# A batch's ranks follow its logits by four steps in place of ten, and its sends stand five steps apart

## The chip, the core and the metric

The kernel runs on one core of a Trainium2 chip. The core has five engines that each work through a queue of their own in order: TensorE (PE, with its weight loads as PEld), VectorE (DVE), ScalarE (ACT), GpSimd (POOL) and SyncE (SP). They wait for each other by semaphores. An instruction that waits holds everything behind it in its queue. Sixteen DMA engines move data for all of them. The metric is the device time of one execution, in microseconds; the times of a kernel are given as the median of several runs, with the lowest and the highest.

## The reference

Attention over 8 batches, 8 heads, 576 tokens and a head width of 64, in which scores more than tau below a row's maximum are dropped, and behind it a layer of 8 experts, of which each token goes to the one with the largest logit.

```python
scores = scale * np.matmul(q, k.transpose(0, 1, 3, 2))
thresh = np.max(scores, axis=-1, keepdims=True) - tau
scores = np.where(scores >= thresh, scores, -1000000000.0)
...
x = np.ascontiguousarray(attn_out.transpose(0, 2, 1, 3)).reshape(B * S, H * D)
logits = x @ w_gate
expert_idx = np.argmax(logits, axis=1)
...
for e in range(E):
    mask = expert_idx == e
    xe = x[mask]
    h = np.maximum(xe @ w1[e], 0.0)
    out[mask] = gate_w[mask, None] * (h @ w2[e])
```

## The kernel before

**Stages.** Attention runs over 32 pairs of heads (four pairs are a batch), ten steps to a pair; the loop `one_step` writes out, step after step, what each engine is to do, and the order of each engine's queue is this order. In step t of pair n, TensorE makes one tile of transposed scores (`st_unit`, L444), a piece of the product with v for the pair before (`av_rest`, `av_wide`), and one tile of plain scores for the pair after the next (`s_unit`, L388). VectorE reduces each plain tile to its row maxima (L411, L404) and masks each transposed tile (L481, L463); ScalarE takes exponentials (L478, L462) and rounds (L488); GpSimd makes the low halves (`pl`, L489). When the maxima of a pair are complete, VectorE takes their minimum (`r`, L418), TensorE transposes it (`pst`, L423, at the front of step 2) and ScalarE and VectorE split it into rows that go into CQ by DMA.

**What sets the order.** `after(k, f, where)` (L251) puts a piece of work k steps later, into one of four places of that step: FRONT, BET (after the transposed scores), MID (after the plain scores), END. `chain` (L258) spreads a list two to a step, `dense` (L263) three to a step. `phase(p, least)` (L254) gives the first distance of at least `least` steps that ends at step p of a pair.

**Logits, ranks and sends.** About 25 steps after a batch's last evacuation, at step 6 of a pair, `logits` (L670) makes the batch's logits on TensorE (32 matmuls for four tiles of tokens, 40 where a fifth tile holds the last 64 tokens of two batches), into `lg`. One step later `route` (L688) starts: eight VectorE pieces (L704 to L712) find each token's expert as a one-hot tile `oh` and add to the running counts `run`. `ranks` (L732) stands nine steps after `route`, at step 6 of the next pair: five or six matmuls turn `oh`, and the counts before this batch, into each token's place among its expert's tokens (`rk`), and seven VectorE pieces (L744 to L753) make of it the row number `posi` and the gate's denominator `sm`; `gate` (L728) writes the gate into the rows. Six steps after the ranks the first of the batch's sends follows (L760): an indirect DMA of GpSimd that writes 128 rows of `R` (or `Rh`, the fifth tile) to `xs` in DRAM at the rows of `posi`. The sends of batches 0 to 4 stand four steps apart, those of batch 5 two.

**Buffers around it.** `ps_m` (tag `m`) is one bank of PSUM: `pst` of every pair, `lg` and `rk` of every batch use it in turn, each after all readers of the one before. `R` has two buffers, so a batch writes its rows (L613, L610) into the one that the sends of two batches ago read. After each odd batch a lone tile (`lone`, L636) is divided and rounded on GpSimd (xnh L572, Rh L647) and transposed on SyncE's queue (L663).

**Behind attention** come the experts: rows are fetched from `xs` by tables made of the counts, and TensorE works through two matrix products per group of rows. The first tables (`tables0`) and fetches follow batch 5.

Of the kernel before, what the change touches and what calls it, by code (L numbers as in the profile page):

```python
# [15 lines left out]
ALU = mybir.AluOpType  # L16
# [4 lines left out]
B, H, S, D = 8, 8, 576, 64  # L21
# [26 lines left out]
TUNE = dict(  # L48
    lgp=6, rkp=6, hi=4, lo=5, rd=5, lead=10, r0=2, rs=1, r2=1, pl=0, pa=3, q0=1, qd=1, lgs=2, rks=2, c1=2, c3=1, c5=1, sl=10, ll=13, sp0=8, sps=0, lv=-9, sv=5, t0=16, av=2, tr=4, d=4, lg=5, d5=2, d6=2, d7=1, lg7=22, km=16, rate=15, dh=1, do=3, w1d=5, xv=3, so=0, sto=0, ord=0, sc=5, fa=3, fd=4, wa1=-70, w2=38, wa2=-86, wl1=-28, wl2=-6, avb=2, route=1, ranks=7, pp=8, ew=4, maskat=0, w1a=-35, w0=14, w1b=3,
)  # L50
# [3 lines left out]
def kernel(  # L54
# [196 lines left out]
    def after(k, f, where=END):  # L251
        plan(now[0] + k, f, where)

    def phase(p, least):  # L254

        return least + (p - now[0] - least) % NSTEP if now[0] + least < KM else least
# [431 lines left out]
    def route(b, n, dist, Lj, w, got):  # L688
# [6 lines left out]
        def t2(nm, dt=F32):  # L695
# [6 lines left out]
        nc.scalar.copy(was, run)  # L702
        (dense if b == B - 1 else chain)(0, [
            lambda: nc.vector.tensor_reduce(mx, Lj, axis=AX.X, op=ALU.max),  # L704
# [27 lines left out]
        def ranks():  # L732
# [4 lines left out]
            for i in range(n - 1):  # L737
# [5 lines left out]
            pos, total = (rk[:, z:z + n].unsqueeze(2) for z in (128, 136))  # L743
            after(0, lambda: tt(ps, rkv, base_e.unsqueeze(1).to_broadcast(bc), ALU.add), END)  # L744
            fs = [
                lambda: nc.vector.tensor_reduce(total, ex, axis=AX.X, op=ALU.add),
# [8 lines left out]
                lambda: gate(b, n),  # L755
            ]
            (dense if b == B - 1 else chain)(1, fs)

            def send(j):
                dma = nc.gpsimd.indirect_dma_start(  # L760
                    xs[:, :], bass.IndirectOffsetOnAxis(ap=posi[:, j:j + 1].bitcast(U32), axis=0), row(b, j), None
                )
                tc.declare_no_dep(dma.ins, group="xs", reason="each row of xs is written once, and read later")
                tc.add_to_no_dep_group("xs", dma.ins)
                sends.append(dma.ins)
                sent.add((b, j))
# [3 lines left out]
            for j in range(n):  # L770
                after(6 + dist * j, lambda j=j: send(j))

        after(phase(TUNE["rkp"], TUNE["ranks"]), ranks, TUNE["rks"])


# [511 lines left out]
    at = []  # L1287
# [200 lines left out]
```

## Time and profile before

| | |
|---|---|
| median of 3 runs | 914.24 us (906.66 to 915.16) |
| profiled execution | 911.92 us, of it 910.2 us span |
| TensorE clock granted over the span | 0.997 |
| TensorE busy | 872.8 us (96%) |
| VectorE, ScalarE, GpSimd busy | 638.2, 614.6, 547.1 us |
| HBM read and written | 90.56 and 19.17 MB |

Attention takes the first 500 us or so, the experts the rest. In the views below, times are microseconds from the start of the span; a row of the timeline gives an instruction's start, its length, its engine and line, what it writes and reads, and in square brackets how long the engine stood idle ahead of it and what ended that. The matmuls' ends are modelled, so their starts say more than their lengths.

### The profile page before, as it was taken

To read this page: it belongs to the slowest core of one execution; us is meant where nothing else is said; L and a number is where in the kernel's file an instruction comes from. 1 tells how busy PE (TensorE), PEld (TensorE's weight loads), DVE (VectorE), ACT (ScalarE), POOL (GpSimd) and SP (SyncE) were. 2 spreads that over 40 slices of the span, in tenths; PEclk is the share of its full clock that TensorE was granted. 3 is DMA by queue.
4 is the path that set the end of the run, shared out by engine and by line. 5 is a ranking of instruction groups with operands and counts; after the bars stand their busy time and mean duration, and the time that the engine had idled before them with its cause. 6 is when DMAs were issued, how large, how long until landed. Compare 5 with 4: busy or idle time off the path is not lost.

```text
span 910.2 us, 25378 instructions
## 1 busy us (share of the span) xinstructions
PE 872.8 (96%) x10047; PEld 626.9 (69%) x10047; DVE 638.2 (70%) x1322; ACT 614.6 (68%) x1074; POOL 547.1 (60%) x471
## 2 busy tenths in 40 slices
PE   4899999999999999999999999999999999999996
PEld 1377777777777677777777867676666666667773
DVE  7999999989899899898988746745334251524551
ACT  4799999989999899999889624453334252433561
POOL 7578888998989889989889634323222122221132
PEclk9999999999999999999999999999999999999999
DMA  8555666666866767867457785999755664646540
GB/s 198 142 126 124 152 145 150 163 160 144 202 149 166 161 149 167 170 149 187 110 146 191 190 193 181 314 302 339 189 174 160 185 190 144 192 146 218 188 168 27
DMA packets 176981, 158.16 MB, mean 174 GB/s; under 512 B 133273, under 2 KB 149147, under 8 KB 176860
## 3 DMA queue, kind: packets, MB, share of 16 engines
q1 hardware_dynamic: 156028, 105.39, 45.8%
q0 software_dynamic: 8992, 29.18, 10.2%
q10 hardware_dynamic: 11840, 21.94, 9.0%
q8 instruction: 80, 1.31, 0.6%
q14 instruction: 41, 0.34, 0.1%
HBM read 90.56 MB, written 19.17 MB: 121 GB/s over the span
## 4 chain that ended last, share of the span: by engine, by line
PE 36%; issue 5%; DMA 5%; POOL 4%; DVE 2%; ACT 2%; SPq 1%; ACTq 0%; POOLq 0%; DVEq 0%
PE h L380 16%; PE y L380 15%; DMA out_dram<-o,gt 2%; DMA xs<-R,posi 1%; POOL out_dram L1122 1%; DMA vf<-in_v_dram 1%; SPq L663 1%; DMA wf<-in_w_dram 1%; POOL xs L760 1%; POOL pl L493 1%; PE st L450 1%; PE s L395 1%; PE s L399 1%; PE st L380 1%; POOL xn L572 0%
## 5 line engine op out<-in xcount | busy, mean ns | idle before, releaser
L489 POOL TENSOR_TENSOR pl<-e,ph 128x1024 f16<-128x1024 f32 x93 | 198.6, 2136 | 51.3 <-ACT ph L488 45.4
L411 DVE TENSOR_REDUCE nm<-s 128x1 f32<-128x512 f32 (+1 forms) x320 | 199.9, 634 | 9.5 <-PE s L399 7.9
L380 PE MATMUL y<-wb,hl 128*128 128x512 f16 (+2 forms) x1104 | 196.3, 347 | 0.9 <-DVE hl L1071 0.8
L380 PEld LDWEIGHTS <-wb 128*128 128x128 f16 x2304 | 182.9, 98 | 19.7 <-issue 1.5
L975 DVE SCALAR_TENSOR_TENSOR wb<-wf,wb 128x1024 f16<-128x1024 f32 x96 | 119.4, 1276 | 73.5 <-ACT wb L972 70.7
L380 PE MATMUL h<-xT,wb 128*128 128x256 f16 (+3 forms) x1632 | 160.8, 260 | 0.3 <-issue 0.3
L380 PEld LDWEIGHTS <-hl 128*128 128x128 f16 (+2 forms) x1104 | 89.0, 98 | 98.9 <-DVE hl L1071 1.4
L481 DVE SCALAR_TENSOR_TENSOR e<-st,e 128x512 f32<-128x512 f32 x192 | 129.8, 676 | 23.4 <-ACT e L478 23.1
L395 PE MATMUL s<-QK 128*128 128x512 f16 (+3 forms) x640 | 133.1, 291 | 12.5 <-POOL QK L137 8.0
L450 PE MATMUL st<-QK 128*128 128x512 f16 (+3 forms) x640 | 136.0, 288 | 4.2 <-DVE e L481 2.0
L972 ACT ACTIVATE wb<-wf 128x1024 f16<-128x1024 f32 x96 | 98.3, 1053 | 60.0 <-DMA wf<-in_w_dram 46.7
L399 PE MATMUL s<-ck,CQ 128*128 128x512 f16 (+3 forms) x640 | 137.4, 290 | 0.0
L478 ACT ACTIVATE e<-st,ntau 128x512 f32<-128x512 f32 x192 | 132.3, 692 | 7.3 <-PE st L380 3.9
L1122 POOL DMA_INDIRECT out_dram<-o,gt x39 | 44.6, 1143 | 147.3 <-ACT o L1119 138.5
L380 PE MATMUL st<-CQ,ck 128*128 128x512 f16 (+3 forms) x640 | 131.1, 286 | 1.1 <-DMA CQ<-ptT 1.0
L541 PEld LDWEIGHTS av<-vf,e 128*128 128x128 f32 x512 | 91.8, 190 | 19.6
L462 ACT ACTIVATE e<-st,ntau_f 128x512 f32<-128x512 f32 (+1 forms) x160 | 92.3, 608 | 13.8 <-PE st L380 9.5
L488 ACT CAST ph<-e 128x1024 f16<-128x1024 f32 x93 | 96.6, 1038 | 5.9 <-issue 3.2
L1070 ACT ACTIVATE hl<-h 128x512 f16<-128x512 f32 (+2 forms) x78 | 43.6, 573 | 80.6 <-PE h L380 78.5
L561 PE MATMUL av<-vop,pl 128*128 128x65 f16 x768 | 97.2, 194 | 0.5 <-issue 0.5
L560 PE MATMUL av<-vop,ph 128*128 128x64 f16 x768 | 97.0, 193 | 0.3 <-issue 0.3
L562 PE MATMUL av<-vop,ph 128*128 128x65 f16 x768 | 96.0, 193 | 0.7 <-issue 0.7
(234 smaller groups left out, 1538.0 us busy)
## 6 DMA issues: line engine op xcount, KB each, us to landing
wf<-in_w_dram SPq DMA_DIRECT2D x96, 512.0 KB
QK<-z SPq DMA_DIRECT2D x124, 144.0 KB
qkf<-in_qk_dram ACTq DMA_DIRECT2D x29, 576.0 KB
vf<-in_v_dram SPq DMA_DIRECT2D x31, 320.0 KB
ck<-z SPq DMA_DIRECT2D x62, 72.0 KB
CQ<-z ACTq DMA_DIRECT2D x58, 72.0 KB
xT<-R SPq DMA_TRANSPOSE x153
x<-in_qk_dram SPq DMA_DIRECT2D x6, 288.0 KB
```

Source lines behind the costliest of these rows:

```text
L380: x = nc.tensor.matmul(*a, **kw).ins
L395: nc.tensor.matmul(sc[rows, oc], d["QA"][a][:, cols], d["KB"][a][:, CH[c]], start=True, stop=False)
L399: nc.tensor.matmul(sc[rows, oc], d["CQ"][:, at:at + cols.stop - cols.start], d["CK"][a][:, CH[c]], start=False, stop=True,)
L411: nc.vector.tensor_reduce(o, sc[:, 0:width(t)], axis=AX.X, op=ALU.max, negate=True)
L450: nc.tensor.matmul(sc[rows, oc], d["KB"][a][:, cols], d["QA"][a][:, CH[c]], start=True, stop=False)
L478: nc.scalar.activation(pf, sc, AF.Exp, bias=ntau, scale=0.125 / SS)
L481: masks.append(nc.vector.scalar_tensor_tensor(pf, sc, 0.0, pf, ALU.is_ge, ALU.mult).ins)
L489: nc.gpsimd.tensor_tensor(l, pd, h, ALU.subtract)
L560: nc.tensor.matmul(av[:, a, 0:D], h, vop[:, tv, W:W + D], start=False, stop=False)
L561: nc.tensor.matmul(av[:, a], l, vop[:, tv, 0:W], start=False, stop=False)
L972: high = nc.scalar.activation(o[:, :, 0], x, AF.Copy, scale=SW)
L975: low = nc.vector.scalar_tensor_tensor(o[:, :, 1], x, SW, o[:, :, 0], ALU.mult, ALU.subtract)
```

## The change

Four things move, for batches 0 to 5 (`soon`); nothing is computed otherwise.

- `route` writes its eight pieces three to a step in place of two, in every batch.
- The ranks stand three steps after `route` (`phase(0, 3)`), at step 0 of the next pair, behind its first transposed scores: four steps after the logits in place of ten.
- Their eight VectorE and ScalarE pieces stand in the order 0, 1, 2, 4, 6, 3, 5, 7 within this step and the next, instead of over four steps.
- The first send stands four steps after the ranks in place of six, and the others five steps apart (batch 5: four) in place of four (two).

```diff
-    ... tr=4, d=4, lg=5, d5=2, d6=2, ...
+    ... tr=4, d=5, lg=5, d5=4, d6=2, ...
...
-        (dense if b == B - 1 else chain)(0, [
+        dense(0, [
...
-            after(0, lambda: tt(ps, rkv, base_e.unsqueeze(1).to_broadcast(bc), ALU.add), END)
-            fs = [
+            fs = (
+                lambda: tt(ps, rkv, base_e.unsqueeze(1).to_broadcast(bc), ALU.add),
                 lambda: nc.vector.tensor_reduce(total, ex, axis=AX.X, op=ALU.add),
                 lambda: tt(ps, ps, oh, ALU.mult),
                 lambda: nc.vector.tensor_scalar(sm, total, 1e-9, None, ALU.add),
...
-            ]
-            (dense if b == B - 1 else chain)(1, fs)
+            )
+            if soon(b):
+                for i, at, where in (
+                    (0, 0, MID), (1, 0, END), (2, 0, END), (4, 1, FRONT), (6, 1, FRONT), (3, 1, BET), (5, 1, MID), (7, 1, END)
+                ):
+                    after(at, fs[i], where)
+            else:
+                after(0, fs[0], END)
+                (dense if b == B - 1 else chain)(1, fs[1:])
...
-                after(6 + dist * j, lambda j=j: send(j))
-
-        after(phase(TUNE["rkp"], TUNE["ranks"]), ranks, TUNE["rks"])
+                after((4 if soon(b) else 6) + dist * j, lambda j=j: send(j))
+
+        if soon(b):
+            after(phase(0, 3), ranks, BET)
+        else:
+            after(phase(TUNE["rkp"], TUNE["ranks"]), ranks, TUNE["rks"])
+
+    def soon(b):
+        return b < B - 2
```

VectorE's queue around the transpose at step 2 of the pair after batch 0's logits. Before, from the third mask ahead of `r` (a name's number is its buffer's; `e` and `st` are transposed scores, `nm` and `s` plain ones):

```order
L463 SCALAR_TENSOR_TENSOR e_6_2709<-st_6_2706,e_6_2709 128x512
L708 TENSOR_REDUCE mw_2675<-lg_2624 128x4
L411 TENSOR_REDUCE nm_2419<-s_7_2737 128x1
L709 TENSOR_TENSOR oh_2676<-lg_2624,mw_2675 128x32
L463 SCALAR_TENSOR_TENSOR e_6_2709<-st_7_2731,e_6_2709 128x512
L711 TENSOR_REDUCE lg_2624<-oh_2676 128x8
L712 TENSOR_TENSOR run<-run,lg_2624 128x8
L418 TENSOR_REDUCE r_2742<-nm_2419 128x9
L411 TENSOR_REDUCE nm_2768<-s_0_2769 128x1
L481 SCALAR_TENSOR_TENSOR e_0_2760<-st_0_2757,e_0_2760 128x512
L411 TENSOR_REDUCE nm_2768<-s_1_2798 128x1
```

and now, from `r` (the ranks' lines L744 and L746 to L753 are L745 and L746 to L753 in the changed kernel):

```order
L418 TENSOR_REDUCE r_2745<-nm_2419 128x9
L411 TENSOR_REDUCE nm_2776<-s_0_2777 128x1
L745 TENSOR_TENSOR rk_2768<-rk_2768,base_e 128x32
L746 TENSOR_REDUCE rk_2768<-ex_2677 128x4
L747 TENSOR_TENSOR rk_2768<-rk_2768,oh_2676 128x32
L481 SCALAR_TENSOR_TENSOR e_0_2763<-st_0_2760,e_0_2763 128x512
L749 TENSOR_REDUCE rk_2768<-rk_2768 128x4
L752 CAST posi_2680<-rk_2768 128x4
L753 COPY pos_165<-rk_2768 128x1
L748 TENSOR_SCALAR sm_2678<-rk_2768 128x4
L411 TENSOR_REDUCE nm_2776<-s_1_2812 128x1
L750 RECIPROCAL sm_2678<-sm_2678 128x4
```

The ranks' readers now stand between `r` and the second reduction of the pair, and L708 to L712 stand together, two masks and a reduction earlier.

GpSimd's queue from the pair after batch 0's logits, before:

```order
L572 TENSOR_TENSOR xn_2755<-y_2754,rs_2753 128x512
L489 TENSOR_TENSOR pl_0_2762<-e_0_2760,ph_0_2761 128x1024
L349 TENSOR_SCALAR full_2945<-vf_113 128x384
L489 TENSOR_TENSOR pl_2_2813<-e_2_2811,ph_2_2812 128x1024
L352 TENSOR_TENSOR vop_110<-full_2945,vop_110 128x6x64
L304 TENSOR_TENSOR z_2820<-qkf_2694,z_2820 128x2x576
L610 TENSOR_TENSOR R_195<-xn_2755,R_195 128x4x128
L489 TENSOR_TENSOR pl_4_2968<-e_4_2966,ph_4_2967 128x1024
L760 DMA xs<-R_194,posi_2680 36864x514
```

and now:

```order
L572 TENSOR_TENSOR xn_2758<-y_2757,rs_2756 128x512
L767 DMA xs<-R_194,posi_2680 36864x514
L489 TENSOR_TENSOR pl_0_2765<-e_0_2763,ph_0_2764 128x1024
L349 TENSOR_SCALAR full_2962<-vf_113 128x384
L489 TENSOR_TENSOR pl_2_2829<-e_2_2827,ph_2_2828 128x1024
L352 TENSOR_TENSOR vop_110<-full_2962,vop_110 128x6x64
L304 TENSOR_TENSOR z_2836<-qkf_2695,z_2836 128x2x576
L610 TENSOR_TENSOR R_195<-xn_2758,R_195 128x4x128
L767 DMA xs<-R_194,posi_2680 36864x514
L489 TENSOR_TENSOR pl_4_2985<-e_4_2983,ph_4_2984 128x1024
```

The first send of the batch stands in this pair instead of at its end, and the second is where the first was, one product earlier.

## Rows read from the trace of the kernel before

**Rows 1.** The page: busy time, share of the span and instructions of each engine.

```profile
PE 872.8 (96%) x10047; PEld 626.9 (69%) x10047; DVE 638.2 (70%) x1322; ACT 614.6 (68%) x1074; POOL 547.1 (60%) x471
```

**Rows 2.** Two pairs, then five cycles of four: start:end, length, each engine's busy us.

```profile
59.04:73.31 14.27, 14.27 (x198) 10.76 (x197) 13.13 (x28) 13.53 (x26) 10.60 (x7) 1.00 0.53 129
73.31:87.59 14.28, 14.28 (x198) 10.76 (x197) 12.98 (x27) 12.97 (x24) 11.83 (x8) 1.00 0.55 133
131.02:191.35 60.33, 59.32 (x826) 44.23 (x824) 54.20 (x122) 55.65 (x105) 53.72 (x36) 1.00 0.67 160
191.35:250.65 59.30, 58.96 (x835) 44.56 (x836) 54.79 (x121) 56.00 (x108) 54.10 (x35) 1.00 0.70 162
250.65:311.87 61.22, 59.43 (x827) 44.33 (x826) 54.34 (x122) 56.00 (x107) 56.42 (x38) 1.00 0.69 163
311.87:371.31 59.44, 59.19 (x834) 44.59 (x835) 54.96 (x121) 56.13 (x109) 53.31 (x35) 1.00 0.71 160
371.31:432.51 61.20, 59.50 (x827) 44.23 (x826) 54.21 (x122) 55.71 (x106) 55.61 (x38) 1.00 0.71 164
```

**Rows 3.** The same view for batch 0's logits (first: TensorE, VectorE) and ranks.

```profile
137.50:141.00 3.50, 0.95 (x32) 0.41 (x2) 1.00 0.74 166
152.00:155.00 3.00, 0.28 (x5) 0.19 (x1) 1.00 0.76 167
```

**Rows 4.** GpSimd's timeline over the first cycle: start, length, instruction, idle time before.

```profile
152.32 2.14 POOL L489 TENSOR_TENSOR pl<-e,ph 128x1024 f16<-128x1024 f32 x1 [2.32 <-ACT ph L488]
154.54 1.17 POOL L349 TENSOR_SCALAR full<-vf 128x384 f32<-128x384 f32 x1
...
164.51 1.21 POOL L760 DMA_INDIRECT xs<-R,posi  x1 [0.18 <-PE st L380]
...
180.72 1.01 POOL L760 DMA_INDIRECT xs<-R,posi  x1 [0.16 <-PE s L399]
...
182.98 1.01 POOL L760 DMA_INDIRECT xs<-R,posi  x1 [0.17 <-issue]
...
197.93 2.14 POOL L489 TENSOR_TENSOR pl<-e,ph 128x1024 f16<-128x1024 f32 x1 [1.18 <-ACT ph L488]
```

**Rows 5.** Who waited for whom, 60 to 480 us: total, times, longest.

```profile
ACT R L613 <- DMA xs<-R,posi: 1.8, 3, 0.8
...
PE pst L423 <- DVE r L418: 1.6, 2, 1.2
...
SPq L663 <- POOL Rh L647: 12.7, 3, 5.1
```

**Rows 6.** VectorE's timeline from batch 0's route to the transpose.

```profile
141.20 0.69 DVE L411 TENSOR_REDUCE nm<-s 128x1 f32<-128x512 f32 x1 [0.90 <-PE s L399]
...
143.90 0.18 DVE L708 TENSOR_REDUCE mw<-lg 128x4 f32<-128x32 f32 x1
143.99 0.68 DVE L411 TENSOR_REDUCE nm<-s 128x1 f32<-128x512 f32 x1
...
145.29 0.21 DVE L711 TENSOR_REDUCE lg<-oh 128x8 f32<-128x32 f16 x1
145.53 0.16 DVE L712 TENSOR_TENSOR run<-run,lg 128x8 f16<-128x8 f16 x1
145.61 0.17 DVE L418 TENSOR_REDUCE r<-nm 128x9 f32<-128x18 f32 x1
145.69 0.68 DVE L411 TENSOR_REDUCE nm<-s 128x1 f32<-128x512 f32 x1
146.29 0.68 DVE L481 SCALAR_TENSOR_TENSOR e<-st,e 128x512 f32<-128x512 f32 x1
```

**Rows 7.** VectorE's timeline at the last batch's ranks, written densely before too.

```profile
549.24 0.20 DVE L744 TENSOR_TENSOR rk<-rk,base_e 128x40 f32<-128x40 f32 x1
549.47 0.20 DVE L746 TENSOR_REDUCE rk<-ex 128x5 f32<-128x40 f32 x1
549.59 1.22 DVE L975 SCALAR_TENSOR_TENSOR wb<-wf,wb 128x1024 f16<-128x1024 f32 x1
```

**Rows 8.** TensorE's timeline at the transpose after batch 0's logits.

```profile
145.97 0.38 PE L399 MATMUL s<-ck,CQ 128*128 128x512 f16 x1
146.18 0.27 PE L423 MATMUL pst<-ident,r 128*9 128x128 f32 x1
```

More of the change, by code (lines that the diff above doesn't have):

```diff
@@ L48 @@
 TUNE = dict(
-    lgp=6, rkp=6, hi=4, lo=5, rd=5, lead=10, r0=2, rs=1, r2=1, pl=0, pa=3, q0=1, qd=1, lgs=2, rks=2, c1=2, c3=1, c5=1, sl=10, ll=13, sp0=8, sps=0, lv=-9, sv=5, t0=16, av=2, tr=4, d=4, lg=5, d5=2, d6=2, d7=1, lg7=22, km=16, rate=15, dh=1, do=3, w1d=5, xv=3, so=0, sto=0, ord=0, sc=5, fa=3, fd=4, wa1=-70, w2=38, wa2=-86, wl1=-28, wl2=-6, avb=2, route=1, ranks=7, pp=8, ew=4, maskat=0, w1a=-35, w0=14, w1b=3,
+    lgp=6, rkp=6, hi=4, lo=5, rd=5, lead=10, r0=2, rs=1, r2=1, pl=0, pa=3, q0=1, qd=1, lgs=2, rks=2, c1=2, c3=1, c5=1, sl=10, ll=13, sp0=8, sps=0, lv=-9, sv=5, t0=16, av=2, tr=4, d=5, lg=5, d5=4, d6=2, d7=1, lg7=22, km=16, rate=15, dh=1, do=3, w1d=5, xv=3, so=0, sto=0, ord=0, sc=5, fa=3, fd=4, wa1=-70, w2=38, wa2=-86, wl1=-28, wl2=-6, avb=2, route=1, ranks=7, pp=8, ew=4, maskat=0, w1a=-35, w0=14, w1b=3,
 )
```

## The prediction

> **What bounds the kernel now.** I read the head of the page first. TensorE is busy for 96% of the span, VectorE for 70% [rows 1], and in the slices up to about 480 us, where the change acts, TensorE shows 9 throughout. That digit hides short stalls, so I went on to the stretches between two of its transposes (L423, one for each pair of heads, always at the same place of a pair), which are the lengths of pairs and of cycles of four pairs [rows 2]. An undisturbed pair takes 14.27 and 14.28 us. A cycle of four has 57.1 us of that, and one batch's logits and ranks on top: 0.95 us for 32 logit matmuls (40 in a batch with five tiles: 1.2) and 0.28 us for ranks [rows 3]. So 58.3 us are needed with four tiles and 58.6 with five. The five cycles take 60.33, 59.30, 61.22, 59.44 and 61.20: too long by 2.0, 0.7, 2.9, 0.8 and 2.9, together 9.3 us. TensorE's own work bounds this part, and what an edit can win is at most these 9.3 us; what it makes TensorE wait is lost whole, since TensorE has no idle time that could take it in. Even batches lose 2.6 us in the mean, odd ones 0.75.
>
> The view of GpSimd over the first cycle tells why even ones lose more [rows 4]. It has 2.32 us of idle time before the cast difference at 152.32, and then hardly any until 197.93. In between lie batch 0's four sends (164.51 to 182.98) and the lone tile's two products of batch 1 (xnh, Rh), which only follow an even batch. The last two sends are pushed together, 2.3 us apart. The list of waits has their price [rows 5]: ScalarE's copy into R (L613) waits 1.8 us, in 3 places, for a send that still reads the R of two batches ago, and three times the transposes of SyncE wait for Rh, 12.7 us in all.
>
> **The sends.** The number of instructions stays, on each engine; 27 sends (four or five in each of batches 0 to 5) cost GpSimd about 1.0 us and an issue of 0.16 each, as before [rows 4]. What moves is where: two of a batch's sends go into the pair after its logits, whose idle 2.32 us hold them, and none is left in the pair of Rh. If that cover were gone, 2.3 us of lag would go on into the next pair, as now. The last send of a batch of four stands five steps earlier, 5 x 1.43 = 7 us, so that L613 finds its R free. SyncE's and ScalarE's DMAs keep their places. I value this at what makes an even cycle worse than an odd one: 2.0 + 2.9 + 2.9 - 3 x 0.75 = 5.5 us. Bounds: nothing (the crowd only moves to an earlier pair, where batches 0, 2 and 4 have a product of 1.17 us, `full`, that the pair after has not), and 9.3 us (all excess). I take 5.5, which is what rows of the same kernel reach with a batch's sends and no lone tile beside them.
>
> **The logits' eight VectorE instructions** now stand three to a step. From 141.20 VectorE has no idle time up to the transpose [rows 6], so the order costs what small instructions cost. Behind a large one that they don't need they take 0.10 us from start to start (143.90 to 143.99); behind a small one whose result they read, 0.24 (145.29 to 145.53), and in the last batch, which is already written this way, 0.23 (549.24 to 549.47) [rows 6, 7]. Two more such pairs in the new order, L708-L709-L711, make VectorE later by 2 x 0.13 = 0.26 us at L418. TensorE's rank matmuls need L712 (they take the one bank of `ps_m` that the logits hold). L712 moves ahead of two masks and a reduction, 3 x 0.60 us; it ends near 144.3, TensorE gets there at 144.4. Cost 0, at most 0.2 a batch.
>
> **The ranks** are the expensive part. `rk` and the pair's transpose `pst` share that bank (`bufs=1`). Before, the last reader of `rk` (L752) stands ahead of L418, on which the transpose waits anyway. In the new order `rk` is filled at step 0 and `pst` is to be written at the front of step 2, so the transpose waits for L748, the last reader, and every later matmul stands behind it on TensorE, and behind these the exponentials and masks. How late is L748? In the trace of before, TensorE starts the transpose at 146.18, 0.49 us after VectorE began L411 for step 0, at 145.69 [rows 6, 8]: VectorE follows nearly two steps behind. In the new order it comes to L748 only after that L411, five small instructions and a mask:
>
> L411 at 145.69 + 0.26 = 145.95; + 0.60 L745; + 0.23 L746; + 0.23 L747; + 0.12 the mask L481 (549.47 to 549.59); + 0.60 L749; + 0.23 L752; + 0.10 L748, at 148.06; + 0.15 its length: 148.2. TensorE arrives at 146.18 + 0.28 for the ranks, now ahead of it: 146.45. **It waits 1.8 us.** Low bound, with 0.10 for every small instruction and no 0.26: 147.5, so 1.1 us. I take 1.8, since the rows at 549 are the same instructions with the same waits. It happens once in each of batches 0 to 5: 10.8 us (low 6.6). Nor is there hidden room elsewhere: the list has transposes waiting 1.6 us for L418 as it is, in two places [rows 5].
>
> The Trainium skill (VectorE: DVE Perf Modes, "The DRAIN you can't avoid") says that a chain of instructions with a semaphore after each takes no longer than one without, so by it bunching costs nothing and the low sum holds. This trace disagrees: 0.23 and 0.24 us behind a result against 0.10 beside other work [rows 6, 7].
>
> ScalarE's gate (L728) follows L750, some 0.5 us after L748; L570 and the exponentials of step 2 queue behind it, but their matmuls are themselves held by the transpose until 148.2 and end 0.5 us later. I cost it at 0; without the transpose's wait it would be up to 0.5 us in ScalarE, a batch. The exponential L733 is ready before L746. Batch 6 only gets the dense logits: 0. Tables and fetches of batch 5 start in the same step: 0.
>
> **Sum**, against the profiled execution, 911.92 us (span 910.2, 1.7 around it): 911.9 + 10.8 - 5.5 = 917.2. It stands 2.3 under the median of the runs shown, 914.24 (906.66 to 915.16); I predict for the profiled one. 1% is 9.1 us, about what a measurement of this kernel can tell from no change.
>
> **Rivals.**
> - *B, the crowd only moves.* GpSimd takes two sends beside `full` in the pair after the logits and two beside xnh in the next, and is as late as now; no gain. For it: it is busy without a break for 28 us once sends and lone work meet [rows 4]. Against: the 2.32 us, and the Rh pair loses both its sends. 911.9 + 10.8 = 922.7, slower by 1.2%. It decides once less than 1.7 us of the 5.5 come back.
> - *C, the wait is paid back.* While TensorE stands, VectorE, ScalarE and GpSimd go on; entering the busy pairs 1.8 us less late, they cause none of the later stalls, in odd cycles neither. 911.9 + 10.8 - 9.3 = 913.4.
> - *D, bunching is free*, by the rule named above: waits of 1.1 us. 911.9 + 6.6 - 5.5 = 913.0. For it only that small rows overlap large ones; against it the two rows with 0.23 and 0.24.
> - *E, no wait.* VectorE is not behind where ranks are read, as where it sat idle 0.90 us for TensorE at 141.20 [rows 6]. Then only the sends count: 906.4. Against: 4.5 us after that idle time it is 1.5 steps behind, in the trace itself.
>
> **How the numbers follow.** My case 0.47, B 0.20, C 0.14, D 0.10, E 0.05, and 0.04 for more than B (a later L418 in several batches). Predicted 917. The range reaches from C and D with some room down to B with some up: 909 to 924; E and the worst are left out. Slower by over 1% (above 921): B, the worst and a tenth of my case, 0.28. Faster by over 1% (below 902.8): none of the cases, 0.02. Within 1%: 0.70.
>
> **What would show it.** Right: in the changed trace TensorE's L423 waits some 1.8 us on VectorE's L748, six times, 0.1 us after L748 ends; the first cycle grows by 1.8 minus what the sends give; no wait of L613 on xs; Rh's waits on SyncE shorter; GpSimd without the 2.3 us gap in the pair after the logits. Wrong: transposes that start within 0.5 us of their predecessors (E), waits near 1.1 us (D), even cycles that still exceed odd ones by 2 us (B), or all cycles at 58.4 us plus the wait (C). The forecast fails if TensorE stops at the rank matmuls too, or if a later copy or load is held by the new place of a send.

## The result and the profile after

The changed kernel takes 925.87 us (median of 15 runs, 921.39 to 929.34); 15 runs of the kernel before beside it took 915.29 us (906.66 to 922.52). The ratio is 1.0114 (95% interval 1.0088 to 1.0140): **slower by 1.1%**, against a forecast of 917 us and a range up to 924. The profiled execution after is the median run itself (925.87 us, span 924.2). The one of before, with a span of 910.2, lies 3.4 us under its own median over these 15, so the traces differ by 14.0 us and the medians by 10.6. Chips differ as well (the kernel before had medians from 915 to 926 us on those used here), so every kernel below is given as a ratio to the kernel before on the same chip. Ratios are formed of the runs within 1.5% of the fastest of the same kernel, which leaves out none of the 15 and 15 here, but leaves of late_ranks, below, only 4 of 10 and of the kernel before beside it 16 of 31.

Where the 14.0 us arise: stretches between the same instructions of the two traces (transposes L423; 497.64 and 512.44 are the same product with v, in the last pair).

| stretch | before | after | difference | forecast |
|---|---|---|---|---|
| start to the cycle of batch 0's ranks | 131.02 | 130.35 | -0.67 | 0 |
| five cycles of four pairs, five stops | 301.49 | 307.41 | +5.92 | 5 x 1.8 - 5.5 = +3.5 |
| batch 5, one stop | 46.36 | 49.16 | +2.80 | +1.8 |
| **handover to the experts** | 18.77 | 25.52 | **+6.75** | 0 |
| the rest | 412.56 | 411.76 | -0.80 | 0 |

The same five cycles as in [rows 2], and the two stretches behind them, in the view by stretches (start:end, length, then busy us and instructions of TensorE, its weight loads, VectorE, ScalarE, GpSimd, and the granted clock, DMA share, GB/s):

```profile
130.35:191.39 61.04, 58.63 (x826) 43.92 (x825) 55.55 (x122) 56.27 (x106) 54.45 (x36) 1.00 0.66 158
191.39:252.53 61.14, 59.05 (x836) 44.18 (x835) 55.63 (x121) 55.90 (x110) 54.80 (x37) 1.00 0.70 162
252.53:313.63 61.10, 58.76 (x827) 43.81 (x825) 55.24 (x122) 56.00 (x106) 54.70 (x36) 1.00 0.65 159
313.63:375.13 61.50, 59.26 (x836) 44.32 (x835) 55.87 (x121) 56.06 (x109) 54.75 (x37) 1.00 0.69 159
375.13:437.76 62.63, 60.28 (x826) 44.72 (x825) 55.33 (x122) 56.24 (x106) 54.48 (x36) 0.97 0.61 153
437.76:486.92 49.16, 44.57 (x636) 33.25 (x636) 42.94 (x100) 38.86 (x81) 38.73 (x28) 1.00 0.51 124
486.92:512.44 25.52, 20.68 (x290) 15.74 (x291) 22.96 (x46) 21.06 (x42) 21.32 (x17) 0.87 0.78 169
```

Two things are to be seen. The first three cycles are level, at 61.0 to 61.1 us: even ones are no longer the long ones (61.2 and 59.4 before), so the sends gave back what they could, but each cycle now holds a stop. And the stretch of the handover has a granted clock of 0.87. In the trace of before it is shorter and at full clock:

```profile
478.87:497.64 18.77, 17.70 (x290) 13.89 (x291) 16.40 (x39) 18.53 (x36) 17.80 (x14) 1.00 0.77 183
```

Who waited for whom, 60 to 480 us (total, times, longest), against [rows 5]:

```profile
ACT R L728 <- DVE sm L750: 13.5, 6, 2.3
...
PE pst L423 <- DVE sm L748: 11.9, 6, 2.0
...
SPq L663 <- POOL Rh L647: 3.7, 2, 1.9
```

The transpose waits for L748 in six places; the wait of L613 for sends is gone, and Rh's waits on SyncE fell from 12.7 to 3.7 us. The row above the transpose's, ScalarE's gate (L728) behind VectorE's L750, is as long, and I had costed it at nothing. VectorE's timeline at the first of the six stops, and TensorE's row, against [rows 6, 8]:

```profile
145.46 0.16 DVE L418 TENSOR_REDUCE r<-nm 128x9 f32<-128x18 f32 x1
145.54 0.68 DVE L411 TENSOR_REDUCE nm<-s 128x1 f32<-128x512 f32 x1
146.13 0.19 DVE L745 TENSOR_TENSOR rk<-rk,base_e 128x32 f32<-128x32 f32 x1
146.43 0.20 DVE L746 TENSOR_REDUCE rk<-ex 128x4 f32<-128x32 f32 x1
146.66 0.20 DVE L747 TENSOR_TENSOR rk<-rk,oh 128x32 f32<-128x32 f32 x1
146.76 0.68 DVE L481 SCALAR_TENSOR_TENSOR e<-st,e 128x512 f32<-128x512 f32 x1
147.36 0.19 DVE L749 TENSOR_REDUCE rk<-rk 128x4 f32<-128x32 f32 x1
147.58 0.16 DVE L752 CAST posi<-rk 128x4 int32<-128x4 f32 x1
147.66 0.15 DVE L753 COPY pos<-rk 128x1 f32<-128x1 f32 x1
147.73 0.15 DVE L748 TENSOR_SCALAR sm<-rk 128x4 f32<-128x4 f32 x1
```

```profile
148.03 0.27 PE L423 MATMUL pst<-ident,r 128*9 128x128 f32 x1 [2.03 <-DVE sm L748]
```

L748 ends at 147.88, and TensorE goes on 0.15 us later. Start to start, the step into the transpose is 2.12 to 2.19 us longer in the six places.

The second loss is one the forecast did not have. (The first experiment below shows that the kernel before has it too, in some executions.) At the handover, where the scheduler and no longer the loop of steps sets the order, VectorE, GpSimd and TensorE show:

```profile
501.05 5.73 DVE L988 SCALAR_TENSOR_TENSOR wb<-wf,wb 128x1024 f16<-128x1024 f32 x1
506.70 0.22 DVE L683 TENSOR_REDUCE lg<-lg 128x32 f32<-128x64 f32 x1
506.83 0.68 DVE L481 SCALAR_TENSOR_TENSOR e<-st,e 128x512 f32<-128x512 f32 x1
```

```profile
500.21 2.14 POOL L489 TENSOR_TENSOR pl<-e,ph 128x1024 f16<-128x1024 f32 x1
502.32 0.18 POOL L1049 TENSOR_TENSOR gt<-Rm,badi 128x1 int32<-128x1 int32 x1
502.46 1.15 POOL L610 TENSOR_TENSOR R<-xn,R 128x512 f16<-128x512 f32 x1
503.58 2.11 POOL L489 TENSOR_TENSOR pl<-e,ph 128x1024 f16<-128x1024 f32 x1
```

```profile
507.56 0.27 PE L450 MATMUL st<-QK 128*64 128x64 f16 x2 [3.60 <-DVE e L481]
```

L988 splits a chunk of the first expert's weights. Alone it takes 1.22 us ([rows 7] has that length for L975, its line before). Here it takes 5.73, and ends 1.09 us after the last of four GpSimd instructions that follow each other without a gap. The mask L481 stands behind it, and TensorE stops for 3.60 us. In the trace of before the same instruction met the same GpSimd instruction, but got through after it:

```profile
491.94 2.22 DVE L975 SCALAR_TENSOR_TENSOR wb<-wf,wb 128x1024 f16<-128x1024 f32 x1
```

```profile
490.94 2.14 POOL L489 TENSOR_TENSOR pl<-e,ph 128x1024 f16<-128x1024 f32 x1
493.04 1.17 POOL L1036 TENSOR_TENSOR gt<-Rm,badi 128x1 int32<-128x1 int32 x1
```

It ended at 494.16, 1.08 after GpSimd's 493.08, and it was GpSimd's next instruction that took 1.17 us in place of 0.18. The two engines exclude each other here. The Trainium skill (SBUF — State Buffer, "Who interferes with whom") says so: a VectorE instruction with two inputs in SBUF (L988 reads wf and wb) shares a read port with GpSimd instructions that read SBUF, and the one that comes second is blocked to the end of the first. The trace agrees with that, 1.09 us behind GpSimd's end in place of 1.22 alone; that the blocked one can be passed over three more times is this trace's.

Behind both kinds of stop the granted clock may fall (view by stretches):

```profile
394.00:396.00 2.00, 2.00 (x18) 1.57 (x17) 1.36 (x3) 1.80 (x3) 0.51 (x1) 0.50 0.87 194
...
506.00:512.00 6.00, 4.44 (x54) 3.93 (x54) 5.97 (x18) 3.34 (x8) 2.90 (x4) 0.50 0.72 175
```

0.50 is the lower of TensorE's two levels, 1.2 GHz. Behind the fifth stop (392.75) it lasts some 3 us, and the pair that follows takes 15.92 us in place of 14.28: 1.64 more. At the handover it begins within TensorE's stop and lasts until 512.5: from the end of the stop (507.56) to the same product with v (512.44) TensorE takes 4.88 us, against 2.43 before (495.21 to 497.64), 2.4 more.

### The profile page after: what moved, and what is told of

Its sections match the earlier page's. It is cut to its first block, busy times and chain, and to the rows that moved or that the text cites. A ratio compares the mean times of both kernels' runs of the same rounds, so it can differ in the third digit from the quotient of the medians.

```text
span 924.2 us, 25352 instructions
## 1 busy us (share of the span) xinstructions
PE 876.5 (95%) x10047; PEld 628.1 (68%) x10047; DVE 646.5 (70%) x1322; ACT 616.4 (67%) x1074; POOL 547.5 (59%) x471
## 3 DMA queue, kind: packets, MB, share of 16 engines
q8 instruction: 80, 1.31, 0.6%
## 4 chain that ended last, share of the span: by engine, by line
PE 34%; issue 5%; DMA 5%; POOL 3%; DVE 3%; ACT 2%; SPq 1%; ACTq 0%; POOLq 0%; DVEq 0%
PE h L380 16%; PE y L380 15%; DMA out_dram<-o,gt 2%; DMA wf<-in_w_dram 1%; DMA xs<-R,posi 1%; POOL pl L493 1%; POOL out_dram L1135 1%; DVE e L481 1%; SPq L663 1%; DMA xT<-R 1%; DVE nm L411 0%; DVE wb L988 0%; PE st L450 0%; POOL xs L767 0%; PE st L380 0%
## 5 line engine op out<-in xcount | busy, mean ns | idle before, releaser
L489 POOL TENSOR_TENSOR pl<-e,ph 128x1024 f16<-128x1024 f32 x93 | 198.3, 2136 | 50.6 <-ACT ph L488 43.1
L411 DVE TENSOR_REDUCE nm<-s 128x1 f32<-128x512 f32 (+1 forms) x320 | 200.0, 635 | 12.7 <-PE s L399 9.4
L988 DVE SCALAR_TENSOR_TENSOR wb<-wf,wb 128x1024 f16<-128x1024 f32 x96 | 121.1, 1293 | 74.6 <-ACT wb L985 71.8
L481 DVE SCALAR_TENSOR_TENSOR e<-st,e 128x512 f32<-128x512 f32 x192 | 129.6, 675 | 25.8 <-ACT e L478 25.0
```

The source lines that it names most:

```text
L411: nc.vector.tensor_reduce(o, sc[:, 0:width(t)], axis=AX.X, op=ALU.max, negate=True)
L481: masks.append(nc.vector.scalar_tensor_tensor(pf, sc, 0.0, pf, ALU.is_ge, ALU.mult).ins)
L489: nc.gpsimd.tensor_tensor(l, pd, h, ALU.subtract)
L988: low = nc.vector.scalar_tensor_tensor(o[:, :, 1], x, SW, o[:, :, 0], ALU.mult, ALU.subtract)
```

## The experiments

**Is it the order or one execution?** Both kernels once more, unchanged.

> The changed kernel a second time. Its first trace shows two losses: six stops of TensorE's transpose (L423) of 2.1 us each behind VectorE's L748, and one stop of 3.6 us at 503.9 us, where VectorE's split of a weight chunk (L988) takes 5.73 us instead of 1.22, with a granted clock of 0.5 for 7 us behind it. Theory 1 (the order of instructions makes both): six stops of 2.1 us again, an L988 of over 4 us between 495 and 510 us and a stop of TensorE over 2.5 us behind it again, span about 924. Theory 2 (the long L988 is an accident of one execution): six stops again, no L988 over 2.5 us there, span about 918.

> The kernel before a second time. Theory 1 (its order lets the same split, L975 there, through after at most one GpSimd instruction): no L975 over 2.5 us between 480 and 500 us, no stop of TensorE over 1.5 us there, span 908 to 916. Theory 2 (accident): an L975 there of over 4 us is as likely as in the changed kernel, and then a stop of some 3 us.

The changed kernel: span 927.8, six stops of 2.12 to 2.19 us, L988 with 5.72 us at 502.14 behind the same four GpSimd instructions, TensorE stopped behind it, the clock at 0.50 from 507. Theory 1, but for one thing: none of its six stops in attention was followed by a fall of the clock.

The kernel before: span 927.4, where Theory 1 had 908 to 916. Its handover is as long as the changed kernel's:

```profile
481.78:508.16 26.38, 20.50 (x291) 15.56 (x290) 21.96 (x40) 20.47 (x39) 20.29 (x17) 0.80 0.61 143
```

Its first two splits (L975) take 2.72 and 5.08 us, TensorE stops for 1.31 and 4.57 us behind them (to 493.18 and 499.37), and the clock is at 0.50 for some 10 us from 495.5. (A stop of 3.76 us ahead of that, to 476.37, has another origin: ScalarE's L346 waits 4.43 us for a load of v.) So the handover's loss is not the changed kernel's alone: the kernel before has it in some executions, with the same order of instructions on VectorE and GpSimd as in its first trace. It is not the same chunk: there the third one's split, here the second one's, which starts behind L352 and is passed by L489, L1036 and L610.

```profile
493.64 5.08 DVE L975 SCALAR_TENSOR_TENSOR wb<-wf,wb 128x1024 f16<-128x1024 f32 x1
```

```profile
493.39 0.91 POOL L352 TENSOR_TENSOR vop<-full,vop 128x384 f16<-128x384 f32 x1
494.25 2.14 POOL L489 TENSOR_TENSOR pl<-e,ph 128x1024 f16<-128x1024 f32 x1
496.33 0.20 POOL L1036 TENSOR_TENSOR gt<-Rm,badi 128x1 int32<-128x1 int32 x1
496.47 1.16 POOL L610 TENSOR_TENSOR R<-xn,R 128x512 f16<-128x512 f32 x1
```

The same stretch, from the last transpose to the same product with v, in all traces:

| ranks and the third split | handover, us |
|---|---|
| new place, L988 in its place: the changed kernel three times, and five variants below | 25.4 to 26.2 (L988: 5.72 or 5.73, in ranks_only 6.56) |
| old place, third split in its place: before, late_ranks | 18.8, 19.2 (third split: 2.2) |
| old place, third split in its place: before_again, logits_only | 26.4, 25.9 (second split: 5.1) |
| old place, third split moved: before_split, late_split | 26.8, 26.9 (second split: 5.1) |
| new place, third split moved: split_later, both_and_split | 19.4, 21.0 |

With the ranks at their old place some executions get through and some do not; with the new place none of eight did. So the 6.75 us of the table above are the distance to an execution of the kernel before that got through, and not what the change costs in every execution. In the two old-place traces that got through, the first chunk's split starts 1.0 to 1.1 us ahead of GpSimd's L572 and takes 1.2 to 1.3 us; in the four others it starts 0.6 us ahead and takes 2.7. What sets that distance was not tried.

**What do the sends give?** Ranks and logits as changed, sends back at their old steps (and d=4, d5=2 again).

```diff
-                after((4 if soon(b) else 6) + dist * j, lambda j=j: send(j))
+                after((12 if soon(b) else 6) + dist * j, lambda j=j: send(j))
```

> The changed kernel with its sends back at the steps of the kernel before (12 steps behind the ranks, four apart, two apart in batch 5); logits and ranks stay where the change puts them. My theory (the stops cost, the sends give back): six stops of 2.1 us, and cycles of four pairs as uneven as before, even ones 1.5 to 2.5 us longer than odd ones; up to 480 us some 12.8 us later than the kernel before, against 8.1 in the changed kernel; that is 4 to 5 us slower than the changed kernel in all. Rival C (the stops themselves leave GpSimd and the others time to catch up, wherever the sends stand): six stops, even cycles level with odd ones, up to 480 us some 8 us late, and the time of the changed kernel within 2 us.

Ratio 1.0258 (1.0181 to 1.0335), the slowest of all. The same five cycles:

```profile
131.40:193.94 62.54, 59.60 (x827) 44.05 (x825) 55.38 (x122) 56.11 (x105) 53.83 (x36) 1.00 0.65 155
193.94:257.20 63.26, 60.94 (x835) 45.08 (x836) 55.75 (x121) 56.24 (x107) 53.86 (x35) 0.97 0.65 152
257.20:320.79 63.59, 59.85 (x827) 44.06 (x827) 55.86 (x122) 56.51 (x107) 56.32 (x38) 1.00 0.63 157
320.79:382.28 61.49, 59.17 (x834) 44.27 (x835) 56.14 (x121) 56.24 (x108) 53.27 (x35) 1.00 0.67 155
382.28:446.00 63.72, 61.07 (x827) 44.88 (x825) 55.46 (x122) 56.33 (x107) 55.13 (x38) 0.97 0.65 156
```

314.60 us in all, 7.2 more than the changed kernel; 1.64 of that is one more fall of the clock (two stops here have one, one there). So the sends' new places are worth 5.5 us in these cycles (4.8 and 5.0 against the changed kernel's two other traces, which have no fall there). Rival C falls: stops alone give next to nothing back. Without the falls the cycles are 9.8 us longer than before, and five stops are 10.7. The whole time missed the expectation, though: not 4 to 5 but some 15 us over the changed kernel (944.69 against 929.52, one run of it on the same chip). Between the two traces 8.0 us of that lie in the five cycles and 4.9 behind the handover; the second part is unexplained.

**Is it the bank?** The ranks need `ps_m` for one VectorE instruction only. A second form then lets the reduction write whole numbers, which takes away a cast.

```diff
-            nc.tensor.matmul(rkv, ones, was.unsqueeze(1).to_broadcast(bc), start=False, stop=True)
-            ps = rk[:, 64:64 + n * E].rearrange("p (j e) -> p j e", e=E)
-            pos, total = (rk[:, z:z + n].unsqueeze(2) for z in (128, 136))
+            for x in (was, base16):
+                nc.tensor.matmul(rkv, ones, x.unsqueeze(1).to_broadcast(bc), start=False, stop=x is base16)
+            ps, pos, total = t3("psb"), t2("pob"), t2("tob")
...
-                lambda: tt(ps, rkv, base_e.unsqueeze(1).to_broadcast(bc), ALU.add),
+                lambda: tt(ps, rkv, oh, ALU.mult),
```

> The changed kernel, in which the ranks need PSUM's bank for one VectorE instruction only: the experts' bases are added by one more small matmul, the product with the choice goes to SBUF, and what follows reads it there (L747 falls away). Same places, same sends. My theory (the transpose waits because the bank is held to L748, 1.6 us behind L745): the six stops shrink from 2.1 to about 0.5 us each, six times 1.65 us or some 10 us less than the changed kernel: about 914 to 916, with the loss near 504 us still there. Rival (VectorE is late for another reason, the transpose would wait as long for L418 or the next instruction): stops of 1.5 us or more, within 3 us of the changed kernel.

> early_release once more, with its own new cost taken out: there the cast of the places (L754), which now read SBUF, took 1.19 us in place of 0.16, ending 1.1 us behind GpSimd's instruction, in all five batches of the stretch. Here the reduction writes whole numbers itself and the cast falls away: 15 small VectorE instructions a batch for 17. Theory V (VectorE's work in the pair sets the loss, and the bank only decides which TensorE instruction stops): in the pair of the ranks 1.8 us over 14.28, in the pair behind it at most 0.5 (3.4 and 0.0 in the changed kernel, 1.84 and 1.51 in early_release): 1.1 to 1.5 us less a batch, 7 to 9 us less than the changed kernel, about 921 to 923 on this chip. Rival (what the transpose saves is always given back in the next pair): two pairs together 3.3 over again, time as early_release, 930 to 932.

The stops shrank to 0.6 us or less in both, as expected, and the time did not: ratios 1.0132 (1.0063 to 1.0200) and 1.0126 (1.0074 to 1.0177). My expectation of 7 to 10 us failed twice. Pair with the ranks and pair behind it, changed kernel and early_release2:

```profile
130.35:148.03 17.68, 15.65 (x236) 11.55 (x235) 16.29 (x44) 14.67 (x29) 15.19 (x10) 1.00 0.56 128
148.03:162.30 14.27, 14.27 (x198) 10.76 (x198) 13.12 (x27) 13.13 (x25) 10.77 (x8) 1.00 0.60 157
```

```profile
129.99:146.10 16.11, 15.68 (x236) 11.56 (x235) 14.87 (x38) 14.64 (x29) 13.60 (x10) 1.00 0.62 132
146.10:161.76 15.66, 14.82 (x198) 11.01 (x198) 14.96 (x31) 13.04 (x25) 12.29 (x8) 1.00 0.62 152
```

The first pair is 1.57 us shorter, the next 1.39 longer. What stops TensorE there is seen on VectorE and ScalarE of early_release2:

```profile
146.73 1.22 DVE L754 TENSOR_SCALAR sm<-tob 128x4 f32<-128x4 f32 x1
147.87 0.68 DVE L413 TENSOR_REDUCE nm<-s 128x1 f32<-128x512 f32 x1
```

```profile
148.66 0.21 ACT L730 ACTIVATE R<-sm 128x4 f32<-128x4 f32 x1 [2.70 <-DVE sm L756]
148.77 0.20 ACT L572 ACTIVATE rs<-y 128x8 f32<-128x8 f32 x1
148.88 0.67 ACT L480 ACTIVATE e<-st,ntau 128x512 f32<-128x512 f32 x1
```

ScalarE stands 2.70 us ahead of the gate, with the next exponential behind it, until 148.88, which is no earlier than in the changed kernel (148.82), and later if counted from the cycle's first transpose (18.89 against 18.47). Part of that wait is new. With its operands in SBUF, L754 takes 1.22 us for 4 numbers a partition and ends (147.95) with this instruction of GpSimd (147.93):

```profile
145.80 2.13 POOL L491 TENSOR_TENSOR pl<-e,ph 128x1024 f16<-128x1024 f32 x1
```

The reciprocal, and so the gate, stand behind L754. In early_release it was the cast that took 1.19 us; it ended at 148.91, with GpSimd's instruction at 148.87, and not 1.1 us behind it as the expectation above says; in the changed kernel, which reads PSUM there, the two took 0.15 and 0.16.

**Both stops.** The gate two steps later, first alone, then together with the early release; beside them the changed kernel on the same chip.

```diff
-                    (0, 0, MID), (1, 0, END), (2, 0, END), (4, 1, FRONT), (6, 1, FRONT), (3, 1, BET), (5, 1, MID), (7, 1, END)
+                    (0, 0, MID), (1, 0, END), (2, 0, END), (4, 1, FRONT), (6, 1, FRONT), (3, 1, BET), (5, 1, MID), (7, 3, END)
```

In both_waits the reciprocal (5) stands one step later too, and reads the sum itself:

```diff
-                lambda: nc.vector.tensor_scalar(sm, total, 1e-9, None, ALU.add),
-                lambda: nc.vector.reciprocal(sm, sm),
+                lambda: nc.vector.reciprocal(sm, total),
```

> The changed kernel again, as the measure for the other kernels of this call, which run on the same chip. Expected, by the two traces of it: six stops of L423 of 2.1 us, one or none of them with a granted clock of 0.5 behind it, L988 of 5.7 us at about 501 us with the clock at 0.5 behind the stop; 1.0 to 1.4% over the kernel before.

> The changed kernel with ScalarE's gate (L728) two steps later, one step ahead of the first send. In the trace of the changed kernel ScalarE stands 2.30 us ahead of the gate (to 148.59) with the next exponential (L478, 148.82) behind it, while TensorE's transpose stands to 148.03; both follow VectorE's short instructions. Theory G (two stops side by side, each enough by itself): the transposes stop 2.1 us as before, pair with the ranks 3.4 over 14.28, time within 2 us of the changed kernel. Rival (it is ScalarE's stop that costs, the transpose's is covered by it): at least 0.7 us less a batch, 4 us less in all.

> Both stops taken away at once: PSUM's bank is free after the ranks' first VectorE instruction (as in early_release2), ScalarE's gate stands two steps later, and the gate's sum goes into the reciprocal without the 1e-9 (which changes no float32 sum of 1 or more; L754 of early_release2, which took 1.22 us behind GpSimd in place of 0.15, falls away). Theory G: the transpose stops 0.5 us, no stop of ScalarE over 1 us, and the two pairs together are 1.0 to 1.8 us over 28.56 instead of 3.4: 1.6 to 2.4 a batch, 9 to 14 us less than the changed kernel, at or under the kernel before. Rival (what is saved comes back in the next pair all the same, since VectorE has more to do than it can): 3 us or more over in the two pairs, within 3 us of the changed kernel.

The changed kernel again: 1.0187 (1.0073 to 1.0302). The gate alone: 1.0124 (1.0050 to 1.0198), not to be told from it, with the stops at 2.1 us as before, five cycles of 307.46 us, and ScalarE now standing 2.87 us for TensorE in place of VectorE. Both together: 1.0078 (1.0040 to 1.0117), and the two pairs are

```profile
131.58:147.69 16.11, 15.68 (x237) 11.56 (x235) 14.87 (x38) 14.80 (x30) 13.62 (x10) 1.00 0.67 133
147.69:162.12 14.43, 14.43 (x198) 10.82 (x199) 13.27 (x29) 12.73 (x23) 12.22 (x8) 1.00 0.67 165
```

30.54 us in place of 31.95: the next pair's 1.39 is 0.15 now. The five cycles fall from 307.41 to 298.70 us, 2.8 under the kernel before. This is as Theory G has it: two stops stood side by side, and taking one away gave nothing. But the run takes away three things: the bank's wait, the gate's place, and L754 with its 1.22 us. No run has the early release with the gate in its old place and without L754, so how the 1.39 us divide between these two is open. The span fell by less: from 923.1 in the changed kernel's trace on this chip to 918.4. The cycles are 7.6 us shorter there and batch 5 is 1.8, the handover is as long (L988 took 5.73 us at 491.53), and the rest behind it is 4.4 us longer, for no reason found.

**The handover.** The split of the third chunk four masks later on VectorE.

```diff
+        if (e, w, c) == (0, 0, 2):
+            after(3, lambda: tc.add_manual_dep(
+                nc.vector.scalar_tensor_tensor(o[:, :, 1], x, SW, o[:, :, 0], ALU.mult, ALU.subtract).ins, masks[-1].name, BEHIND
+            ))
+            return
         low = nc.vector.scalar_tensor_tensor(o[:, :, 1], x, SW, o[:, :, 0], ALU.mult, ALU.subtract)
```

> The changed kernel, in which VectorE takes the split of the third weight chunk of the first expert (L988, 5.72 us at 501 us in three traces) four masks later. Theory P (L988 waits for the port that GpSimd's four instructions in a row, 500.2 to 505.7 us, hold, and the masks behind it on VectorE stop TensorE): no stop of TensorE over 1.5 us between 497 and 510 us, no granted clock of 0.5 behind it, 3.6 + 2.3 = 5.9 us less than the changed kernel: about 924 on this chip. Rival (the masks are late for another reason, the long L988 only fills the time): stop and time stay within 1.5 us of the changed kernel, about 930.

> both_waits, with VectorE's split of the third weight chunk four masks later, as in split_later. If the two losses are separate ones (ranks: VectorE's bank and gate; handover: the port), the gains add: 3 to 6 us less than both_waits, 13 to 18 less than the changed kernel, 0.2 to 0.8% under the kernel before. If the handover's stop only hits a kernel that comes late to it, no gain over both_waits.

split_later: 1.0015 (0.9980 to 1.0050). The split still took 4.60 us at its new place, and TensorE's stop there was 1.63 us where I had expected less than 1.5, but the clock stayed at 1.00 behind it, and the handover is 6 us shorter:

```profile
489.45:508.89 19.44, 18.19 (x290) 13.95 (x291) 16.75 (x38) 19.20 (x37) 18.54 (x14) 1.00 0.76 171
```

The time is 927.35 us, where about 924 was expected; the changed kernel itself did not run on that chip. (The trace has two falls of the clock in attention, one more than the changed kernel's, so its span of 922.9 hides part of the gain.)

both_and_split: 1.0023 (0.9986 to 1.0061), on the same chip as both_waits with 1.0078: 5 us less, as expected. The two losses are separate and their gains add; with both gone the kernel is level with the one before. Two parts of the expectation missed: it is 11.7 us under the changed kernel and not 13 to 18, and not under the kernel before. Its trace is that of its longest run: up to the end of the handover it is 1.4 us ahead of the first trace of before (496.21 against 497.64), and then takes 428.7 us to the end in place of 412.6, with four falls of the clock between 517 and 582. What makes them was not tried.

**The change in parts, and what is left.**

> The kernel before, with the logits' eight VectorE instructions of batches 0 to 6 three to a step, and nothing else. As forecast (0.13 us behind each of two more results): VectorE 0.26 us later at L418, 0 to 0.3 us a batch, together at most 2 us: within 0.3% of the kernel before. Rival (bunched instructions cost more than their sum, since TensorE's next scores wait for L418's transpose): 0.5 us or more a batch, 3 to 5 us slower.

```diff
-        (dense if b == B - 1 else chain)(0, [
+        dense(0, [
```

0.9961 (0.9910 to 1.0013): no difference to be told. Its five cycles take 303.48 us against 301.49, 0.4 a batch; more than my 0.3, less than the rival's 0.5. Its trace, too, has L975 at 2.71 and 5.07 us in the handover.

> The change without its move of the ranks: logits and ranks stand three instructions to a step, as in the changed kernel, but the ranks ten steps behind the logits, as before, and a batch's sends follow them by four, four apart (two steps earlier than before); batch 5's ranks and sends are those of the kernel before. Theory V (17 small instructions in one pair are more than VectorE's slack of some 1.2 us a pair): no stop of L423 behind L748, no pair over 14.28 + 1.7; up to 480 us as late as the kernel before or up to 4 us less; time within 5 us of the kernel before, 915 to 921. Rival (three small instructions to a step cost, wherever they stand): 1 us or more a batch over the kernel before, 925 or more.

```diff
-            after(phase(0, 3), ranks, BET)
+            after(phase(TUNE["rkp"], TUNE["ranks"]), ranks, BET)
-        return b < B - 2
+        return b < B - 3
```

(with d=4, d5=2.) 0.9975 (0.9912 to 1.0038), no stop of L423 behind L748, five cycles of 300.40 us, a handover of 19.20 us with L988 in its place. The medians of all runs, 928.27 against 926.37 us, show no gain. Three instructions to a step cost little; the ranks' place costs.

> The kernel before, with VectorE's split of the third weight chunk four masks later and nothing else. Theory S (the handover's loss is the changed kernel's own: the kernel before gets through in 2.2 us): within 0.3% of the kernel before. Theory T (the kernel before has it too, in some executions: the split took 2.22 us in its first trace, 5.08 us in its second with the clock at 0.5 behind it): its median falls by 2 to 4 us, 0.2 to 0.5% faster, and its times lie closer together.

> late_ranks (three instructions to a step, ranks where they were, sends two steps earlier), with the split of the third chunk four masks later. If the ranks' place and the handover are the only losses of the changed kernel, this keeps what the sends give and has neither: late_ranks was 0.25% under the kernel before (interval 0.9912 to 1.0038); with Theory T another 2 to 4 us: 0.3 to 0.8% faster than the kernel before. With Theory S: as late_ranks.

before_split: 0.9971 (0.9926 to 1.0016), which settles nothing: in its trace it was the second chunk's split that took 5.07 us, at 492.28, where the edit does not reach, with TensorE's stops of 2.6 and 3.7 us and the clock at 0.50. So the loss does occur with the kernel before's places of ranks and sends, and moving the third chunk does not take it away there. late_split: **0.9917 (0.9871 to 0.9963)**, faster than the kernel before by 0.8%, and so than both: the early sends without the ranks' move, and the later split. How much of it the split brings is not told, since its interval and that of late_ranks overlap, and its trace, that of its longest run (926.98 us), has the second chunk's split at 5.07 us.

## Why the prediction was wrong, step by step

- **What bounds the kernel**: right. TensorE's stops in attention came through whole, and level cycles show that the excess of even ones could be won.
- **The sends, 5.5 us**: right in size; 4.8 to 5.5 by ranks_only. L613's wait and most of Rh's went as said, and the even cycles' excess with them. GpSimd's idle 2.32 us did not go, as the signs had it: there are 1.80 and 1.37 us now (ahead of 150.07 and 153.88), in a pair that a stop has made longer.
- **The ranks, a stop of 1.8 us in six places**: the mechanism was right (the place, the bank, L748, 0.15 us behind its end), the term 0.34 too small. Counted from the cycle's first transpose, L411 starts 0.26 us later than I had it (15.19 against 14.93), since the logits made L418 0.52 us late and not 0.26; the other 0.08 is L753, which I left out. 6 x 0.34 = 2 us. The steps behind a result were 0.30, 0.23 and 0.22 us (146.13, 146.43, 146.66; 147.36, 147.58), so rival D, bunching is free, falls.
- **ScalarE's gate at 0, up to 0.5 a batch without the transpose's stop**: as long as the transpose stops it costs nothing (gate_later), so the sum was not hurt. Uncovered, it and L754's 1.22 us together cost 1.2 us a batch (1.39 against 0.15); the gate's own share was not measured, so whether 0.5 holds is open.
- **The clock**: not in the sum. It fell behind one of the six stops: 1.64 us (behind none in the changed kernel's two other traces).
- **The step that failed: "Tables and fetches of batch 5 start in the same step: 0."** It put the handover at nothing, on top of one execution of 911.92 us, without a row of it: none of the forecast's rows lies between 480 and 545 us. In the changed kernel's trace the handover is 6.75 us longer than in that execution, the largest part of the 8.7 by which 925.9 exceeds 917.2. The steps were the same, but their time was not: TensorE reached the last transpose 8.0 us later, and the order there differs in a few places (L352 stands ahead of the fetches now). What the runs show in place of the 0: at the ranks' new place L988 waits behind GpSimd's run of instructions in eight of eight traces, and moving this one split shortens the handover to 19.4 and 21.0 us and takes 5 us off both_waits. At the old place the same loss, with another split, came in four of six traces, and not in the one that the forecast stood on. So that base was lucky at this place. How much of the 10.6 us between the medians is the handover's stays open; by the means of these traces, 25.6 against 24.0 us, an estimate is 1.6.
- **The rivals.** B (the crowd only moves) gave a time near 923, and C and E less; none had the handover. Without the handover's and the clock's terms the trace would have come to 910.2 + 14.0 - 6.75 - 1.64 = 915.8 span, 917.5 with the 1.7 around it, which is the forecast; but this is partly terms that cancel, measured against an execution that got through the handover: the stops were 2 us dearer, and the start (0.67) and the rest (0.80) came out shorter for no reason that I can give. So part of the agreement is luck. The chance of slower by over 1% was put at 0.28, and that is what came.

What stays open: why GpSimd's next instruction is let in ahead of the waiting VectorE in some places (502.32) and not in others (493.04). The traces show both, with the same instructions on either side.

## What to carry to other kernels

Where an instruction of one engine makes two others wait, removing one of the waits may show nothing: take both away at once before calling the cause wrong. An edit that delays one stage moves everything behind it against engines that are not delayed by as much, so the stretches behind the last edited instruction need a reading too, above all instructions that share a port. A forecast that starts from one execution takes over its luck: two traces of the kernel before would have shown that its handover comes in two lengths. Moving a small operand from PSUM to SBUF can bring a wait of its own (1.22 us in place of 0.15 here).

## What the hardware showed that I had not expected

- VectorE and GpSimd exclude each other for some forms only. Two inputs in SBUF (L988, L975): 1.22 us alone, 1.3 to 6.6 behind GpSimd, ending 1.08 to 1.09 us after GpSimd's instruction. A cast of 4 float32 numbers from SBUF: 1.19; a tensor_scalar on 4: 1.22. Reductions from SBUF stayed at 0.15 to 0.17 beside the same GpSimd instruction (146.57, 146.66 in early_release2), and the reciprocal at 0.18 beside another (502.94 in both_waits, L495).
- A waiting VectorE instruction is not always next: it was passed by three GpSimd instructions within 4.6 us, in ranks_only by four within 5.5.
- The granted clock fell to 0.50 behind 7 of 36 stops of 2.1 us in attention (six traces with six stops each), at 1.6 us or a little more each, and behind none of 24 stops of 0.3 to 0.6 us (four traces).
